# Another table of order offsets for a list-scheduled kernel: a delta-rule recurrence followed by two MLPs

## The chip, the cores and the metric

The kernel runs on one core of a Trainium2 chip. The metric is the device time of one execution in microseconds (us). Engines are called as the profile calls them: PE (TensorE), DVE (VectorE), ACT (ScalarE), POOL (GpSimd) and SP (SyncE, which issues most DMAs).

## The reference

For each of 4 batches and 8 heads a state of 40 x 40 is carried over 768 time steps; the outputs of all heads side by side are the 3072 tokens of width 320 that go through two MLPs:

```python
for t in range(S):
    y[:, :, t] = np.einsum('bhd,bhde->bhe', rt, state)
    Sa = np.einsum('bhde,bhe->bhd', state, at)
    state_decay = state * wt[:, :, None, :] - np.einsum('bhd,bhe->bhde', Sa, bt)
    state = state_decay + np.einsum('bhd,bhe->bhde', vt, kt)
...
x = attn_out.transpose(0, 2, 1, 3).reshape(B * S, H * D)      # 3072 x 320
h = x @ w_in                                                  # 320 x 2048
g = np.where(h >= 1, h, np.where(h <= -1, 0, (h + 1) ** 2 / 4))
x = g @ w_out
g = x @ w_gate                                                # 320 x 1536
out = (g / (1 + np.exp(-g)) * (x @ w_val)) @ w_out2
```

## The kernel before

Time is cut into 12 chunks of 64 steps. A unit n is one chunk of one batch, 48 in all: n = 4 * chunk + batch. The work is described as tasks; each belongs to a stage, which has a letter:

- **d** (`decay_tasks`, 3 groups of 4 chunks): running products of w and their reciprocals, stored to DRAM.
- **p** (`p_tasks`, per unit): scales a, r, k, b by these, splits them into high and low halves, transposes them, forms the chunk's products (matmuls of L889) and stores a part of them as `lsd` (L910).
- **i** (`inv_tasks`, per chunk): reloads `lsd` of all four batches as tile `ub` (L950) and solves the triangular system by 62 small steps on DVE, alternately L961 and L966, then stores the result as `tsd` (L991). Here it is called the solve.
- **m** (`m_tasks`, per unit): loads the solve's result as tile `tt`, forms the corrections (matmuls of L1103, L1110), the output and the new state, and hands the output over as `x` by a DMA transpose (L1019) into the tokens of the chunk (`mx<-x`). Chunk c needs the state of chunk c - 1.
- **a** and **b** (`in1`, `in2`, `outp`): the first and the second MLP, per chunk 8 and 6 pieces; matmuls of L1240 (into `ph`) and L1307 (into `po`).
- **w** and **v** (`wpiece`): weights of the first and of the second MLP; a piece is loaded (L639), unpacked on DVE from 64-bit floats (L644, L648, L654) and split on ACT and POOL or DVE. **z** is some padding on POOL, **o** the last output products.

Nothing loops on the chip: `Plan.run` writes out every engine's order beforehand. `forward` is a list scheduler: an engine that is free takes, among the tasks that are ready, the one with the smallest priority (a time in us); it never leaves an engine free while a task is ready on it. It has a cost for each task, a count of buffers, and a model of the DMA queue: a DMA isn't taken while the modelled queue is more than `lim` + 1.3 us ahead. `backward` does the same from the end, and gives each task the latest time at which it may start; that time is the next priority. So:

```python
bias = [b + self.offset(self.nudge, t) for t, b in zip(self.tasks, bias)]
for n in range(self.rounds):
    plan = self.forward(prio)
    ...
    if n < self.rounds - 1:
        back = self.backward([-s - c for s, c in zip(plan[1], cost)])
        prio = [plan[0] - s - c + b for s, c, b in zip(back, cost, bias)]
best = self.forward([x + self.offset(self.last, t) for x, t in zip(good, self.tasks)])
```

An offset is looked up twice: by stage and unit (`by_chunk`) and by stage and number of the task within its unit (`by_step`); `nudge` acts in every round, `last` once, at the end. A larger offset puts a task behind others that are ready at the same time. On the chip there is no priority: each engine and each DMA queue does its instructions in the order that came out, and waits at semaphores.

Of the kernel before, what the change touches and what calls it, by code (L numbers as in the profile page):

```python
# [15 lines left out]
class Plan:  # L16
# [10 lines left out]
    def __init__(self):  # L27
        self.tasks, self.made, self.pools, self.slots = [], {}, {}, {}
        self.bias, self.unit, self.nudge, self.last = 0.0, ["z", 0, 0], ({}, {}), ({}, {})
        self.lim, self.rounds, self.loose = 1.97, 5, ()  # L30
# [38 lines left out]
    def forward(self, prio):  # L69
# [56 lines left out]
        now, dma, events, done, starts, out = 0.0, 0.0, [], 0, [0.0] * len(ts), []  # L126
        held = {"DVE": 0.0, "Pool": 0.0}
        win, at_win, work, cold = 4096 / 1200, 0, {}, True
        while done < len(ts):
            started = True  # L130
            while started:
                started = False
                for eng in self.ENGINES[:5]:
# [7 lines left out]
                    while any(heaps):  # L141
                        heap = min((h for h in heaps if h), key=lambda h: h[0])
                        i = heap[0][1]
                        t = ts[i]
# [13 lines left out]
                        end = now + t["cost"]  # L158
# [3 lines left out]
                        if eng == "PE":  # L162
# [3 lines left out]
                            if cold:  # L166
                                end = now + t["cost"] * t["slow"]
# [16 lines left out]
                        if t["dma"]:  # L184
                            heapq.heappush(events, (end, -1))
                            dma = max(dma, begin) + t["dma"]
                            end = dma + 2.16
                        else:
                            end += t["lat"]
# [30 lines left out]
    def backward(self, prio):  # L220
# [16 lines left out]
        def lat(t):  # L237
            return 0.99 + t["dma"] if t["dma"] else t["lat"]
# [107 lines left out]
def tile_recurrence__then__gated_mlps(  # L346
# [1000 lines left out]
    def by(tables):  # L1347
# [23 lines left out]
    })  # L1371
    by_step = by({
# [37 lines left out]
    })  # L1410
    by_step = by({
# [178 lines left out]
```

## Time and profile before

| what | us |
|---|---|
| runs shown | 1070.62, 1068.70, 1068.02 (median 1068.7) |
| the profiled execution | 1071.23, of which the span from first to last instruction is 1069.5 |
| PE busy in the span | 879.1 (82%) |
| POOL, ACT, DVE busy | 778.7, 777.5, 658.3 |
| bytes moved by DMA | 147.93 MB, 138 GB/s on average |

A time of a run is some 1.7 us longer than the span. The rows further below are from the profiled execution.

### The profile page before, as it was taken

To read this page: it belongs to the slowest core of one execution; us is meant where nothing else is said; L and a number is where in the kernel's file an instruction comes from. 1 tells how busy PE (TensorE), PEld (TensorE's weight loads), DVE (VectorE), ACT (ScalarE), POOL (GpSimd) and SP (SyncE) were. 2 spreads that over 40 slices of the span, in tenths; PEclk is the share of its full clock that TensorE was granted. 3 is DMA by queue.
4 is the path that set the end of the run, shared out by engine and by line. 5 is a ranking of instruction groups with operands and counts; after the bars stand their busy time and mean duration, and the time that the engine had idled before them with its cause. 6 is when DMAs were issued, how large, how long until landed. Compare 5 with 4: busy or idle time off the path is not lost.

```text
span 1069.5 us, 28784 instructions
## 1 busy us (share of the span) xinstructions
PE 879.1 (82%) x10944; PEld 729.8 (68%) x10944; DVE 658.3 (62%) x1733; ACT 777.5 (73%) x1442; POOL 778.7 (73%) x996
## 2 busy tenths in 40 slices
PE   0331232955986998999999999999999999999998
PEld 0321222734775887887888888888788888888887
DVE  8789896797868375493583846837558385331111
ACT  1694666896986887888878969879698884744322
POOL 4587868786898888978888879888889764533222
PEclk9999985977998999999999999999999999999999
DMA  7976769879899678777686695957878753110000
GB/s 226 208 178 183 209 154 209 200 157 208 186 205 168 134 147 142 151 151 107 148 156 153 138 163 129 163 125 142 143 161 155 110 108 66 51 34 20 9 9 25
DMA packets 386194, 147.93 MB, mean 138 GB/s; under 512 B 344536, under 2 KB 362776, under 8 KB 386056
## 3 DMA queue, kind: packets, MB, share of 16 engines
q1 hardware_dynamic: 367706, 138.50, 62.4%
q10 hardware_dynamic: 18350, 7.61, 4.0%
q8 instruction: 85, 1.39, 0.6%
q14 instruction: 53, 0.43, 0.1%
HBM read 78.25 MB, written 21.52 MB: 93 GB/s over the span
## 4 chain that ended last, share of the span: by engine, by line
PE 55%; DVE 18%; DMA 11%; ACT 7%; POOL 5%; issue 3%; SPq 1%; ACTq 0%; DVEq 0%; POOLq 0%
PE ph L1240 29%; PE po L1307 18%; DMA mx<-x 3%; DVE pg L966 2%; DMA ub<-lsd 2%; DVE ub L961 2%; PE pg L1195 2%; PE px L1092 2%; PE px L1103 1%; DVE px L644 1%; DVE px L648 1%; PE px L1110 1%; DVE wo L654 1%; DVE vss L572 1%; POOL mx L570 1%
## 5 line engine op out<-in xcount | busy, mean ns | idle before, releaser
L1307 PE MATMUL po<-wo,mx 128*128 128x320 f16 x2016 | 310.8, 302 | 2.0 <-POOL mx L570 2.0
L570 POOL TENSOR_TENSOR mx<-mx 128x512 f16<-128x512 f32 x168 | 193.8, 1159 | 123.4 <-ACT mx L1260 112.0
L1307 PEld LDWEIGHTS <-mx 128*128 128x128 f16 x2016 | 190.9, 98 | 70.3 <-POOL mx L570 3.7
L1240 PE MATMUL ph<-mx,w 128*128 128x256 f16 x1536 | 192.1, 278 | 14.3 <-DMA mx<-x 10.8
L1240 PEld LDWEIGHTS <-w 128*128 128x128 f16 x1536 | 150.1, 100 | 39.3 <-issue 12.5
L1276 DVE SCALAR_TENSOR_TENSOR mx<-ph,mx 128x512 f32<-128x512 f32 x96 | 66.2, 689 | 146.9 <-ACT mx L1273 145.9
L1240 PE MATMUL ph<-x2t,wv 128*128 128x256 f16 x1152 | 142.2, 272 | 0.0
L1240 PE MATMUL ph<-x2t,wg 128*128 128x256 f16 x1152 | 140.8, 272 | 0.7 <-ACT mx L1287 0.7
L1260 ACT CAST mx<-mx 128x512 f16<-128x512 f32 x168 | 101.4, 612 | 42.1 <-DVE mx L1290 26.1
L1240 PEld LDWEIGHTS <-wg 128*128 128x128 f16 x1152 | 109.3, 98 | 14.8 <-issue 0.8
L1240 PEld LDWEIGHTS <-wv 128*128 128x128 f16 x1152 | 109.5, 98 | 13.0
L966 DVE TENSOR_TENSOR pg<-pg,ub 128x126 f32<-128x126 f32 (+22 forms) x372 | 96.0, 258 | 9.1
L961 DVE SCALAR_TENSOR_TENSOR ub<-ub,pg 128x126 f32<-128x126 f32 (+22 forms) x372 | 91.8, 247 | 15.8 <-DMA ub<-lsd 5.7
L1290 DVE SCALAR_TENSOR_TENSOR mx<-ph,mx 128x512 f32<-128x512 f32 x72 | 49.5, 688 | 77.1 <-PE ph L1240 66.6
L1272 ACT ACTIVATE mx<-ph 128x512 f32<-128x512 f32 x96 | 56.9, 592 | 41.4 <-PE ph L1240 34.0
L576 POOL TENSOR_TENSOR ldp<-ldp 128x640 f32<-128x640 f32 (+1 forms) x46 | 69.9, 1527 | 5.1 <-ACT ldp L856 3.8
L572 DVE SCALAR_TENSOR_TENSOR vss<-px,vss 32x320 f16<-32x320 f32 x90 | 43.6, 484 | 42.4 <-ACT vss L1135 39.4
L1287 ACT ACTIVATE mx<-ph 128x512 f32<-128x512 f32 x72 | 42.8, 595 | 36.0 <-PE ph L1240 35.2
L1135 ACT ACTIVATE vss<-px 32x640 f16<-32x640 f32 x90 | 61.1, 690 | 6.1 <-PE px L1103 3.6
L572 DVE SCALAR_TENSOR_TENSOR xs<-px,xs 32x320 f16<-32x320 f32 x89 | 42.6, 483 | 36.4 <-ACT xs L1121 34.6
L570 POOL TENSOR_TENSOR wt<-qf,wt 128x512 f16<-128x512 f32 x44 | 50.9, 1157 | 19.2 <-ACT wt L1181 18.1
L1273 ACT ACTIVATE mx<-mx 128x512 f32<-128x512 f32 x96 | 60.5, 630 | 3.0
(237 smaller groups left out, 1714.0 us busy)
## 6 DMA issues: line engine op xcount, KB each, us to landing
ldp<-in_kb_dram SPq DMA_DIRECT2D x21, 320.0 KB
ldv<-in_v_dram SPq DMA_DIRECT2D x21, 320.0 KB
ub<-lsd SPq DMA_DIRECT2D x23, 256.0 KB
ldp<-in_ar_dram SPq DMA_DIRECT2D x18, 320.0 KB
wo<-in_wo_dram SPq DMA_DIRECT2D x14, 320.0 KB
out_dram<-mx SPq DMA_DIRECT2D x24, 160.0 KB
waf<-was SPq DMA_DIRECT2D x23, 160.0 KB
ldp<-was SPq DMA_DIRECT2D x22, 160.0 KB
```

The costliest lines, as they stand in the source:

```text
L570: e.tensor_tensor(out=out, in0=x, in1=hi, op=ALU.subtract)
L572: e.scalar_tensor_tensor(out=out, in0=x, scalar=scale, in1=hi, op0=ALU.mult, op1=ALU.subtract)
L576: e.tensor_tensor(out=out, in0=x, in1=y, op=ALU.mult)
L961: v_.scalar_tensor_tensor(out=t, in0=L()[:, j, j + 1:].unsqueeze(1).to_broadcast([128, nm, ni]), scalar=-(2.0**-10), in1=m[:, 0:nm, j:j + ...
L966: v_.tensor_tensor(out=m[:, 0:nm, j + 1:], in0=m[:, 0:nm, j + 1:], in1=t, op=ALU.add)
L1135: s_.activation(out=hi2(G("vss", key)[z]), in_=two(hd(G("px", key))[32 * hf:32 * hf + 32]), func=AF.Copy, scale=-(2.0**-10))
L1240: t_.matmul(out=ps, lhsT=wts[:, wi, fs], rhs=xT[:, xi, :], start=(i == 0), stop=(i == len(plan) - 1))
L1260: T("ACT", c_s(512) - 0.04, lambda: s_.copy(out=G("g", key)[:, 0], in_=u2(key)), r=[(key, "u")], w=[(key, "gh")], use=U + GG, p=p)
L1272: s_.activation(out=u2(key), in_=ps2(key), func=AF.Relu, scale=2.0**-8, bias=1.0)
L1273: s_.activation(out=u2(key), in_=u2(key), func=AF.Square, scale=2.0**3)
L1276: T("DVE", c_v(512, True), lambda: v_.scalar_tensor_tensor(out=u2(key), in0=ps2(key), scalar=2.0**8, in1=u2(key), op0=ALU.max, op1=ALU.min ...
L1307: t_.matmul(out=ps, lhsT=g[:, x, f, 128 * tt:128 * tt + 128], rhs=wo[:, 2 * i + f, y, :], start=(n == 1 and f == 0 and m == 0), stop=(n == ...
```

## The change

The two tables of offsets, `nudge` and `last`, are replaced in full, and four numbers of the planner change. Tasks, their instructions and the cost that the planner takes for each stay as they are, so the program issues the same operations on the same engines (a plain DMA can come from SP or ACT, as before), in another order. Of the tables the lines below are those of the stages spoken of later; the rest, and both `by_step` tables, are replaced in the same way.

```diff
-        self.lim, self.rounds, self.loose = 1.97, 5, ()
+        self.lim, self.rounds, self.loose = 0.93, 2, ()
...
-                            end = dma + 2.16
+                            end = dma + 2.13
...
-            return 0.99 + t["dma"] if t["dma"] else t["lat"]
+            return 1.05 + t["dma"] if t["dma"] else t["lat"]
...
     by_chunk = by({
-        "a": {0: -1.35, 1: -1.12, 2: -0.89, 3: -0.66, 4: -0.43, 5: -0.2, 6: 0.03, 7: 0.26, 8: 0.49, 9:
-            0.72, 11: 3.5},
-        "b": {0: 1.42, 1: 1.31, 2: 1.21, 3: 1.09, 4: 0.98, 5: 0.87, 6: 0.77, 7: 0.65, 9: 1.65, 10: 0.33,
-            11: 22.69},
-        "d": {0: 4.91, 1: 0.22, 2: 0.14},
-        "i": {0: -29.34, 1: -13.04, 2: -12.55, 3: -14.73, 4: -12.76, 5: -18.16, 6: -17.61, 7: -11.81, 8:
-            -9.63, 9: -10.04, 10: -14.05, 11: -9.06},
-        "m": {9: 0.08, 10: 0.08, 11: 0.08, 12: 0.08, 40: -5.78, 45: -0.28, 46: 0.54, 47: 2.88},
...
-        "p": {0: -0.1, 1: -0.07, 2: -0.05, 3: -0.04, 4: -0.01, 5: 0.01, 6: 0.02, 7: 0.05, 8: 0.07, 9:
-            0.1, 10: 0.11, 11: 0.13, 12: 0.16, 13: 0.18, 14: 0.2, 15: 0.22, 16: 0.24, 17: 0.27, 18:
...
-        "v": {0: -5.36, 1: -5.09, 2: -4.81, 3: -4.54, 4: -4.28, 5: -4, 6: -3.73, 7: -3.46, 8: -3.18, 9:
-            -2.92, 10: -2.65, 11: -2.37, 12: -2.1, 13: -1.83, 14: -1.55, 15: -1.29, 16: -1.01, 17:
-            3.74},
...
+        "a": {0: 7.83, 1: 7.65, 2: 7.68, 3: 7.49, 4: 7.06, 5: 7.33, 6: 6.68, 7: 6.49, 8: 5.94, 9: 6.11,
+            10: 7.98, 11: 5.44},
+        "b": {0: 12.01, 1: 10.99, 2: 10.71, 3: 10.42, 4: 10.09, 5: 9.78, 6: 9.5, 7: 8.93, 8: 2.44, 9:
+            9.89, 10: 13.19, 11: 20.43},
+        "d": {0: -0.4, 1: -0.21, 2: -5.81},
+        "i": {0: 1.32, 1: -6.72, 2: -4.4, 3: 0.58, 4: 6.85, 5: -1.09, 6: -0.93, 7: -4.48, 8: 16.67, 9:
+            -2.48, 10: 26.07, 11: 17.27},
+        "m": {0: -0.98, 1: -0.84, 2: -0.7, 3: -1.59, 4: -0.42, 5: -0.26, 6: -0.16, 7: -0.02, 8: -2.92,
+            9: -1.14, 10: 0.39, 11: 0.53, 12: -0.08, 13: 1.39, 14: 0.95, 15: -0.35, 16: 1.22, 17: 1.35,
...
+        "p": {0: 14.35, 1: 11.23, 2: 11.5, 3: 11.28, 4: 9.91, 5: 9.94, 6: 11.9, 7: 9.51, 8: 10.73, 9:
+            8.22, 10: 10.53, 11: 9.4, 12: 10.37, 13: 15.11, 14: 10.19, 15: 10.1, 16: 10.03, 17: 9.94,
...
+        "v": {0: -4.69, 1: 3.52, 4: -0.75, 5: -2.29, 6: -3.81, 7: -5.32, 8: -6.81, 9: -8.61, 10: -9.88,
+            11: -12.21, 12: -12.96, 13: -14.5, 14: -16.22, 15: -17.73, 16: -19.27, 17: -26.95},
...
     by_chunk = by({
-        "d": {0: 7.57, 1: -3.33, 2: -1.8},
-        "i": {0: -6.38, 1: -0.07, 2: 11.5, 3: -1.04, 4: -35.75, 5: -26.27, 6: -0.34, 7: -0.98, 8:
...
+        "d": {0: 1.14, 1: 0.54, 2: -5.13},
+        "i": {0: -1.72, 1: -2.84, 2: -22.62, 3: -8.62, 4: -10.97, 5: 5.06, 6: 21.81, 7: 1.27, 8: -10, 9:
...
```

Summed over the two `by_chunk` tables (before, then after): stage **a**, chunks 0 to 3: -1.4, -1.2, -0.9, -0.7, then 8.4, 9.5, 7.7, 9.8. Stage **p**, units 8 to 15: 1.6, -2.1, 2.6, -0.2, 1.8, 1.5, 0.5, -0.9, then 10.4, 8.0, 9.5, 9.3, 18.8, 10.6, 9.9, 9.1. Stage **m**, units 8 to 11: 2.5, 4.1, 0.2, 0.1, then -4.7, -0.3, 0.4, -2.9. Stage **i**, chunks 0 to 5: -35.7, -13.1, -1.1, -15.8, -48.5, -44.4, then -0.4, -9.6, -27.0, -8.0, -4.1, 4.0. Stage **v**, pieces 12 to 17: -2.8, -3.3, -3.9, -4.2, -0.3, -0.8, then -16.5, -17.9, 5.6, -19.3, -22.7, -24.3. Stage **d**, group 0: 12.5, then 0.7.

## Rows read from the trace of the kernel before

**Rows 1.** Stages: us busy (count) of PE, PEld, DVE, ACT, POOL; clock, DMA share, GB/s.
```profile
0.00:184.00 184.00, 43.04 (x640) 36.33 (x641) 150.45 (x418) 110.86 (x189) 130.34 (x256) 0.91 0.78 195
184.00:350.00 166.00, 128.10 (x1573) 100.72 (x1570) 136.51 (x333) 137.43 (x263) 135.98 (x158) 0.88 0.89 186
350.00:900.00 550.00, 541.78 (x7092) 455.23 (x7091) 334.13 (x918) 459.01 (x863) 458.41 (x529) 1.00 0.74 140
900.00:1069.50 169.50, 166.17 (x1649) 137.48 (x1647) 37.22 (x65) 70.18 (x130) 54.02 (x55) 1.00 0.10 25
```
**Rows 2.** The chain that ended last, in order of time: start us, us, what.
```profile
241.41 9.18 DMA mx<-x
...
332.94 6.91 DMA mx<-x
339.89 5.32 PE ph L1240 x32
...
409.14 5.95 DMA mx<-x
415.13 5.30 PE ph L1240 x32
...
552.86 4.51 DMA mx<-x
...
1057.79 3.49 PE ph L1240 x32
1061.28 4.91 PE po L1307 x36
```

**Rows 3.** Timeline of PE, where a chunk's MLP or its corrections begin.
```profile
184.27 2.94 PE L1240 MATMUL ph<-mx,w 128*128 128x256 f16 x16
...
250.63 7.55 PE L1240 MATMUL ph<-mx,w 128*128 128x256 f16 x48 [4.87 <-DMA mx<-x]
...
263.11 0.37 PE L1103 MATMUL px<-xs,tt 96*32 96x40 f16 x8
...
304.51 0.39 PE L889 MATMUL pg<-art,kbT 120*128 120x64 f16 x8
...
360.30 0.57 PE L1103 MATMUL px<-xs,tt 96*32 96x40 f16 x16
```

**Rows 4.** DVE busy with L961 alone, in the stretches of five solves.
```profile
69.70:102.10 32.40, 7.54 (x31) 1.00 0.64 163
115.50:160.00 44.50, 7.56 (x31) 0.91 0.61 173
204.60:244.00 39.40, 7.52 (x31) 0.79 0.75 181
317.90:346.30 28.40, 7.56 (x31) 0.82 1.02 183
...
529.70:556.60 26.90, 7.56 (x31) 1.00 0.89 163
```

**Rows 5.** Groups of DVE instructions in the third of these stretches, 204.6 to 244.
```profile
L966 DVE TENSOR_TENSOR pg<-pg,ub 128x126 f32<-128x126 f32 (+21 forms) x30 | 7.8, 259 | 0.5
...
L654 DVE SCALAR_TENSOR_TENSOR wo<-wo,px 128x512 int32<-128x512 int32 (+1 forms) x6 | 3.6, 593 | 0.1
L648 DVE SCALAR_TENSOR_TENSOR px<-wo,px 128x512 int32<-128x512 int32 (+1 forms) x5 | 3.2, 634 | 0.0
L644 DVE TENSOR_SCALAR px<-wo 128x512 int32<-128x512 int32 (+1 forms) x5 | 3.1, 629 | 0.0
```

**Rows 6.** SP's own timeline: the store of the third solve's result.
```profile
249.01 3.52 SPq L991 DMA_DIRECT2D tsd<-ub  x2
```

**Rows 7.** The chain ahead of the fourth solve: start us, us, what.
```profile
307.86 4.66 DMA lsd<-gf
...
313.12 4.80 DMA ub<-lsd
```

**Rows 8.** The same view around the second chunk's handover.
```profile
241.00:251.00 10.00, 1.36 (x12) 0.76 (x11) 9.47 (x26) 4.86 (x11) 6.26 (x8) 0.50 1.11 210
251.00:300.00 49.00, 45.93 (x539) 37.20 (x537) 40.00 (x74) 42.80 (x81) 38.16 (x42) 0.96 0.88 189
300.00:333.00 33.00, 23.58 (x327) 19.17 (x326) 24.73 (x68) 28.58 (x58) 30.04 (x35) 0.95 0.96 205
```

164 rows, old and new, of tables (by_chunk, by_step) are left out of this document.

## The prediction

> **What bounds the kernel now.** I read the busy time by stage first. From 350 us to the end PE is idle for 8.2 of 550 us and 3.3 of 169.5 us; before that for 141 of 184 us and 38 of 166 us [rows 1]. So after 350 us the program is a queue of matmuls with almost no hole, and no order can take more than some 11 us out of it. That this queue runs at PE's pace shows at its end in the chain of waits: 32 matmuls of L1240 in 3.49 us and 36 of L1307 in 4.91 us [rows 2], 109 and 136 ns each; the 3840 and 2016 of them that the page counts are 693 us of the span. What an order can win lies ahead of 350 us: when the first chunks of tokens arrive.
>
> The same chain, read for what PE waits for at the turn of a chunk, names the handover `mx<-x` each time [rows 2]. The first MLP begins chunk 0 at 184.3, chunk 1 at 250.6, chunk 2 at 339.9 and chunk 3 at 415.1 us [rows 2, 3]: distances of 66, 89 and 75 us. By [rows 1] PE is the bound later; the chunk that comes after 89 us is the outlier, and the clock is hurt around it too (0.88 on average from 184 to 350 us, [rows 1]).
>
> Why chunk 2 is late is read by going back from its first correction matmul at 263.1 us [rows 3]. It needs the solve of chunk 2, which ran from 204.6 to 244.0 us [rows 4], 19.1 us ahead; for chunk 3 the same distance is 14.0 us (346.3 to 360.3) [rows 3, 4]. The 62 steps of a solve are 15.4 us of DVE (7.6 for L961, 7.8 for L966) [rows 4, 5], but the solve of chunk 2 was spread over 39.4 us, where later ones take 26.9 to 28.4 [rows 4]. What stood between its steps is largely unpacking of weights: 9.9 us of L644, L648 and L654 [rows 5]. Chunk 3 is fed in a like way: `lsd<-gf` of its last unit at 307.9, `ub<-lsd` at 313.1, and the solve at 317.9 us [rows 4, 7].
>
> **The change, part by part.** No instruction is added or taken away, so the 693 us of MLP matmuls and every engine's busy sum stay. Each part is worth what it does to those handovers.
>
> *Start, up to 184 us.* Stage d, group 0, comes forward by 11.7 us of priority, the solve of chunk 0 loses 35 us of it. The planner never leaves DVE free while something is ready, so another task slips into the gap behind a step whatever the priorities are. Bounds from the solves: the first one takes 32.4 us and could take 26.9 (-5.5) or, like the second, 44.5 (+12.1) [rows 4]. I take 0, since both signs have a reason here.
>
> *Solve of chunk 2.* Its offset goes from -1.1 to -27.0, and units 8 to 11 of stage m from between 0.1 and 4.1 to between -4.7 and 0.4, while stages a and p go back by 8 to 11 us. So the stages that feed chunk 2's handover are preferred on all engines. Bounds: -12.5 (39.4 to 26.9) and +5.1 (39.4 to 44.5) [rows 4]. Against the full gain stands that the last pieces of stage v (12, 13 and 15 to 17) come forward by 14 to 24 us, and their unpacking is what fills this very stretch. I take -6, about half of the better end, nearer to the fourth solve than to the second.
>
> *The store and reload behind it.* On SP the two stores of the solve's result took until 252.5 us (249.0 + 3.52) [rows 6], 8.5 us behind its end. With `lim` at 0.93 the planner holds DMAs back until its modelled queue is shorter by 1.04 us, so an urgent one is passed by fewer of the loads. Bounds: -5.1 (19.1 to 14.0) and 0; I take -1, the difference in `lim`, the row nearest to what is changed.
>
> *The handover transposes.* `mx<-x` took 9.18 and 6.91 us for chunks 1 and 2, 5.95 and 4.51 for chunks 3 and 5 [rows 2]; from 241 to 251 us the DMA engines had no free time (share 1.11) [rows 8]. Bounds: both like the shortest, -7.1, or both like the longest, +2.3. I take -1, by the same reasoning on `lim`. The new figures 2.13 and 1.05 shift modelled times by 0.03 and 0.06 us and I cost them at nothing, as I do `rounds`: fewer rounds change what the offsets are added to, and its effect is that of the offsets.
>
> *Chunks 3 to 5.* PE waits at 409.1 and 552.9 us for a handover again [rows 2], so a chunk 2 that is 8 us earlier pays only if those are earlier too. I count 0 here, that is, they follow: POOL and ACT are busy for 458 and 459 of 550 us [rows 1], which leaves a sixth of their time, some 36 us over the 220 us from 340 to 560, to do 8 us sooner what feeds them. Where this fails is the third rival.
>
> *The end.* Behind the last matmul only an eviction and a store are left, at most the 3.3 us in which PE is idle after 900 us [rows 1]; larger offsets of the last products change nothing there.
>
> Sum: 0 - 6 - 1 - 1 + 0 = -8 us. Against the profiled execution that is 1069.5 - 8 = 1061.5 us of span, 1063.2 us as a time; that execution (1071.23) is 2.5 us over the median of the runs shown, so against the median of 1068.7 it is 1060.7 us. A measurement of this kernel tells about 0.3% from no change, 3.2 us.
>
> **The rivals.** (1) *More of it.* The first solve and that of chunk 2 both come down to the shortest row: -5.5 - 12.5 = -18, 1050.7 us. For it: 38 us of idle PE from 184 to 350 us, and a clock of 0.88 [rows 1], so there is that much to have. Against it: the same DVE work must still be done by then, and DVE is busy for 137 of 166 us.
>
> (2) *Given back at chunk 3.* Chunk 2 comes earlier, chunk 3 does not: PE drains its queue and waits at 409 us for what it gained before. 1068.7 us. For it: PE already stands there until `mx<-x` lands at 415.1 [rows 2], without any reserve. Against: the sixth of free time above.
>
> (3) *Slower: chunk 3 starved by stage p.* Units 12 to 15 of stage p get offsets of 9 to 19, where m has about none and v is at -17 to -24. They feed `lsd<-gf` of chunk 3, which is on the chain at 307.9 us [rows 7] right behind the last product of stage p at 304.5 us [rows 3]; the solve behind it takes 28.4 us already, so it can't catch up [rows 4]. From the first us by which it is later, chunk 3's handover at 415 us is later by as much. Its price is that of the lag against m, 9 to 11 us for three of the four units, less the 1 to 2 us of the DMA terms: +8, 1076.7 us. Against it: the offsets are added to latest start times, and what is on the chain has the earliest of these.
>
> (4) *The clock.* When chunk 1 had to be waited for, PE was at the lower level (granted 0.50 from 241 to 251 us, busy for 1.4 of 10 us) [rows 8], and the first 48 matmuls behind took 7.55 us [rows 3] where 48 x 109 ns are 5.2. If the new order breaks the matmuls from 251 to 333 us up, they fall to that level in part: 69.5 us of busy PE at 0.95 to 0.96 [rows 8] would be 75.4 at 0.88, the mean from 184 to 350 us [rows 1], and 132.7 at 0.50 [rows 8]. I take the first, the nearer row: +6, 1074.7 us. The Trainium skill's page "TensorE: Matmul & The Clock Gate", section "HAM oscillation — how this bites in real kernels", says that waits between bursts make the array fall back to the slow clock, so that each burst starts cold; by that rule moving stages a behind m, with the MLP's matmuls in shorter bursts, speaks against this change, and the time would be this rival's. The trace agrees with it at 250.6 us, by the 7.55 us above. I give it little, because the matmuls of 251 to 300 us, broken up by waits as they are, still ran at 0.96 [rows 8].
>
> **How the numbers follow.** Forecast 0.42, rival 1 0.15, rival 2 0.16, rival 3 0.24, rival 4 0.03. Faster by over 0.3%: 0.42 + 0.15 = 0.57; within: 0.16; slower: 0.24 + 0.03 = 0.27. As both signs hold much, the forecast's own range is 1054 to 1066 us (the solve of chunk 2 at its best, or half of my value with the DMA terms at nothing). The range over the cases reaches from 1047, which leaves out the part of rival 1 in which the DMA terms come on top, to 1078, which leaves out those of rivals 3 and 4 in which a second handover slips too or more of the stretch runs at the lower level: about 0.15 in all.
>
> **What would show it.** Right: the first matmuls of chunk 2 at about 332 instead of 339.9 us, its solve in 34 us or less, chunk 3 at about 407, and as little idle PE after 350 us as now. Given back: chunk 2 earlier, chunk 3 still at 415. Rival 3: `lsd<-gf` of chunk 3 after 308 us and the wait at 409 us longer. Rival 4: a clock below 0.9 from 251 to 333 us. The forecast is wrong altogether if the gain or loss lies before 184 us, where I put nothing, or after 560 us.

## The result and the profile after

The kernel after takes 1059.45 us (median of 6 runs, 1055.21 to 1063.74), the kernel before 1069.66 us beside it (6 runs, 1068.02 to 1074.30): a ratio of 0.9886, interval 0.986 to 0.9913. So it is faster, by 10 us of the medians (9 to 15 us by the interval). The execution that was profiled after is the slowest of its six (1063.74 us, span 1061.6); against the span of before (1069.5) it shows 7.9 us.

The stages, busy us (count) of PE, PEld, DVE, ACT, POOL, then clock, DMA share and GB/s, in the kernel after:

```profile
0.00:184.00 184.00, 48.53 (x708) 40.89 (x709) 152.03 (x421) 116.14 (x199) 132.99 (x253) 0.65 0.78 194
184.00:350.00 166.00, 130.87 (x1604) 103.37 (x1602) 135.65 (x335) 141.81 (x270) 141.20 (x170) 0.93 0.86 194
350.00:900.00 550.00, 540.41 (x7058) 453.86 (x7057) 332.22 (x913) 451.77 (x848) 451.85 (x521) 0.99 0.73 138
```

Against [rows 1] the long middle stretch is as full as it was; PE has run 99 matmuls more by 350 us (2312 for 2213). What moved is when the chunks arrive. The timeline of PE of the kernel after, where a chunk's MLP or its corrections begin (in brackets what PE waited for, and how long):

```profile
177.47 1.88 PE L1240 MATMUL ph<-mx,w 128*128 128x256 f16 x8
...
235.63 1.89 PE L1240 MATMUL ph<-mx,w 128*128 128x256 f16 x8 [8.99 <-DMA mx<-x]
239.34 0.42 PE L1103 MATMUL px<-xs,tt 96*32 96x40 f16 x8 [1.82 <-DMA tt<-tsd]
...
324.83 1.91 PE L1240 MATMUL ph<-mx,w 128*128 128x256 f16 x16 [0.83 <-ACT mx L1287]
...
400.04 1.91 PE L1240 MATMUL ph<-mx,w 128*128 128x256 f16 x16
...
478.69 1.58 PE L1240 MATMUL ph<-mx,w 128*128 128x256 f16 x13
```

Chunk 0 comes 6.8 us sooner than in [rows 3], chunk 1 15.0, chunk 2 15.1 (339.89 to 324.83) and chunk 3 15.1 (415.13 to 400.04). Chunk 4 stood in the kernel before at:

```profile
486.84 2.34 PE L1240 MATMUL ph<-mx,w 128*128 128x256 f16 x20 [0.19 <-DMA mx<-x]
```

So it comes 8.1 us sooner, and that is what is left at the end. Two things are to be explained: where 15 us came from, and where 7 of them went between chunks 3 and 4.

**Where they came from.** DVE busy with L961 alone, in the stretches of the third and the fourth solve, kernel after:

```profile
188.00:223.60 35.60, 7.66 (x31) 0.97 0.85 206
304.00:334.70 30.70, 7.61 (x31) 1.00 0.97 208
```

Beside [rows 4] the solve of chunk 2 starts at 188.0 instead of 204.6 us (-16.6) and lasts 35.6 instead of 39.4 (-3.8). From its end to the first corrections it is 15.7 instead of 19.1 us (-3.4); the corrections are thus 23.8 us sooner. From there to the chunk's MLP it is 85.5 instead of 76.8 us (+8.7). Sum: -15.1. The largest term is the start of the solve, which the prediction did not look at.

The way back from that start leads to 131 us. SP's timeline shows the store `lsd<-gf` of the chunk's last unit and the load `ub<-lsd` with which the solve begins, first before, then after:

```profile
191.31 2.19 SPq L910 DMA_DIRECT2D lsd<-gf  x2
...
198.41 1.18 SPq L950 DMA_DIRECT2D ub<-lsd  x2
```

```profile
177.93 0.80 SPq L910 DMA_DIRECT2D lsd<-gf  x2
...
182.04 1.43 SPq L950 DMA_DIRECT2D ub<-lsd  x2
```

The store waits for stage p, and stage p's unit 9 for one of its buffers: `kbs` is written by ACT at L872 once PE has read the old one at L1195, in the product that gives the outputs of stage m's unit 1. PE's timeline of the kernel before, then of the kernel after (L818 are transposes, L1171 and L1195 products of stage m, L889 the grams of stage p):

```profile
145.59 1.03 PE L818 MATMUL po<-mx,vss 128*128 128x128 f16 x8 [5.22 <-DVE vss L572]
146.41 0.63 PE L1171 MATMUL po<-art,vsT 120*128 120x64 f16 x8
146.86 0.62 PE L889 MATMUL pg<-art,kbT 120*128 120x64 f16 x8
...
150.49 0.57 PE L1195 MATMUL po<-kbs,mx 128*128 128x40 f16 x16 [1.95 <-ACT mx L1181]
151.81 0.37 PE L1195 MATMUL po<-kbs,mx 128*128 128x40 f16 x8 [0.76 <-DVE mx L570]
```

```profile
131.41 0.59 PE L1171 MATMUL po<-art,vsT 120*128 120x64 f16 x8
...
137.88 1.04 PE L818 MATMUL po<-mx,vss 128*128 128x128 f16 x8 [2.05 <-DVE vss L572]
138.94 0.96 PE L1195 MATMUL po<-kbs,wt 128*128 128x40 f16 x24
139.73 0.59 PE L889 MATMUL pg<-art,kbT 120*128 120x64 f16 x8
```

In the kernel before, unit 1's L1171 stood behind the transposes of unit 2, for which PE waited 5.2 us for DVE; its own input had been copied by ACT (L821) by 132 us. After, it runs 15 us sooner and the output product 11.6 us sooner (138.94 for 150.49). ACT refills `kbs` behind it, before and after:

```profile
152.72 0.72 ACT L872 ACTIVATE kbs<-ldp 128x640 f16<-128x640 f32 x1
```

```profile
139.96 0.74 ACT L872 ACTIVATE kbs<-ldp 128x640 f16<-128x640 f32 x1
```

Once unit 9 has its `kbs`, the tile `ldp` is free, into which units 10 and 11 are loaded: SP issues the first of these loads (L838) at 155.56 us before and at 143.69 after. The grams of units 9, 10 and 11 come 8.6, 15.7 and 13.8 us sooner (160.31, 180.45 and 189.20 us before). So the link shown here is the larger part of the 13.4 us at the store (191.31 to 177.93), and some is added behind it.

**Where 7 us went.** SP's timeline of the kernel after at chunk 3, then PE's:

```profile
430.22 0.36 SPq L1040 DMA_DIRECT2D ldv<-in_v_dram  x1
431.04 0.48 SPq L950 DMA_DIRECT2D ub<-lsd  x1
431.70 1.25 SPq L807 DMA_TRANSPOSE vsT<-vss  x1
```

```profile
441.65 0.61 PE L1171 MATMUL pg<-art,vsT 120*128 120x64 f16 x8 [4.32 <-DMA vsT<-vss]
```

A transpose for which PE waits is issued right behind a load of 320 KB and one of 256 KB (ACT's queue issues another 256 KB at 431.85), and in the chain of waits it takes 9.91 us (431.70 to 441.61). PE stands for 4.3 us, and then runs at the lower level for a while (windows of the kernel after):

```profile
431.00:442.00 11.00, 6.68 (x124) 5.66 (x123) 4.32 (x8) 7.74 (x15) 9.49 (x11) 0.92 1.01 135
442.00:446.00 4.00, 4.00 (x28) 2.47 (x26) 2.60 (x9) 1.00 (x3) 1.16 (x1) 0.50 0.32 71
```

### The profile page after: what moved, and what is told of

Its sections match the earlier page's. It is cut to its first block, busy times and chain, and to the rows that moved or that the text cites. A ratio compares the mean times of both kernels' runs of the same rounds, so it can differ in the third digit from the quotient of the medians.

```text
span 1061.6 us, 28722 instructions
## 1 busy us (share of the span) xinstructions
PE 878.0 (83%) x10944; PEld 729.0 (69%) x10944; DVE 656.5 (62%) x1733; ACT 778.6 (73%) x1442; POOL 778.0 (73%) x996
## 4 chain that ended last, share of the span: by engine, by line
PE 60%; DVE 17%; ACT 7%; DMA 7%; POOL 4%; issue 4%; SPq 1%; ACTq 0%; POOLq 0%; DVEq 0%
PE ph L1240 31%; PE po L1307 20%; PE pg L1195 2%; DVE ub L961 2%; DVE pg L966 2%; DMA vsT<-vss 2%; PE px L1092 2%; PE px L1103 2%; DVE px L644 2%; PE px L1110 1%; DVE px L648 1%; POOL mx L570 1%; DVE wo L654 1%; DMA tsd<-ub 1%; DMA tt<-tsd 1%
## 5 line engine op out<-in xcount | busy, mean ns | idle before, releaser
L1240 PEld LDWEIGHTS <-w 128*128 128x128 f16 x1536 | 147.4, 99 | 44.3 <-issue 13.3
L1240 PE MATMUL ph<-x2t,wg 128*128 128x256 f16 x1152 | 144.9, 276 | 2.3 <-DVE mx L1276 2.0
L961 DVE SCALAR_TENSOR_TENSOR ub<-ub,pg 128x126 f32<-128x126 f32 (+22 forms) x372 | 92.0, 247 | 16.5 <-DMA ub<-lsd 6.1
L1103 PEld LDWEIGHTS <-tt 96*128 96x128 f16 (+1 forms) x768 | 28.3, 97 | 46.7 <-issue 26.3
```

The lines of the kernel that those rows point to most:

```text
L961: v_.scalar_tensor_tensor(out=t, in0=L()[:, j, j + 1:].unsqueeze(1).to_broadcast([128, nm, ni]), scalar=-(2.0**-10), in1=m[:, 0:nm, j:j + ...
L1103: t_.matmul(out=out, lhsT=lhsT, rhs=xs[:, h], start=False, stop=(h == H - 1), skip_group_check=True)
L1240: t_.matmul(out=ps, lhsT=wts[:, wi, fs], rhs=xT[:, xi, :], start=(i == 0), stop=(i == len(plan) - 1))
```

## The experiments

Most of them set the two orders beside each other as fixed lists and splice them; the planner is not run anew, since its offsets hold for one plan only: of the 16 ways to mix the old and the new values of the four numbers, the new tables give an order with the four new ones alone. So what the tables bring without the numbers was not tried. The splice follows for T = 110 us, T being a time of the plan; `old` and `new` are the two plans, in runs 6 and 7 they change places, and every buffer is chosen as its own plan chose it. Here and in the later runs, a step that can't have its buffer or its input yet is passed by until it can:

```diff
+    a, b = new, old
+    first = [x for x in a[2] if a[1][x[0]] < 110.0]
+    done = {i for i, _ in first}
+    order = first + [x for x in b[2] if x[0] not in done]
```

**1. new110_old and 2. new180_old** (T = 110 and 180): is it the start, or stage p?

> New order for all tasks that the new plan starts before 110 us, the order of before for the rest. Theory A (the gain is made between 120 and 240 us, where units 9 to 11 of stage p and with them the solve of chunk 2 come sooner): nothing won yet, chunk 2's first matmul at 338 to 342 us as before, time 1066 to 1073 us, ratio to before 0.997 to 1.004. Rival B (the gain comes from the start, stage d and the padding): chunk 2 at 330 us or earlier, 1062 us or less, ratio below 0.993.

> New order up to 180 us, the order of before for the rest. Theory A: the solve of chunk 2 begins near 188 instead of 204.7 us, so most of the lead is there; chunk 2's first matmul at 326 to 333 us, time 1055 to 1063 us, ratio 0.987 to 0.994. Rival C (the lead is made behind 180 us, by fewer DMAs ahead of the handovers and less unpacking inside the solve of chunk 2): chunk 2 at 336 us or later, ratio above 0.996.

Measured: 1079.4 us (ratio 1.0069, 1.0045 to 1.0093), chunk 2 at 345.7; and 1076.99 us (1.0055, 1.0037 to 1.0073), chunk 2 at 342.7. Both are slower than the kernel before, the first also than either theory had it, so the first 110 us bring no gain by themselves. The second is the instructive miss: the grams of stage p for chunk 2 ran at 137.6 to 173.2 us, as soon as in the kernel after, and the solve still started at 209. Its SP timeline shows why:

```profile
175.75 0.80 SPq L910 DMA_DIRECT2D lsd<-gf  x2
...
202.51 1.23 SPq L950 DMA_DIRECT2D ub<-lsd  x2
```

The store is there at 175.8, but the load behind it keeps the place that the old order gave it in the queue, behind stores and weight loads, and is issued 26.8 us later (4.1 in the kernel after). What comes sooner is worth nothing as long as its consumer's load keeps its place.

**3. new240_old, 4. new300_old and 5. new340_old** (T = 240, 300, 340): how much of the stretch is needed?

> New order up to 240 us, so with the whole of chunk 2's solve, the order of before for the rest. Theory A, narrowed by the cut at 180 us (stage p of chunk 2 was 16 us sooner there, but the load for its solve kept its old place in the queue, and nothing was won): with the solve in its new place it begins near 188 us and chunk 2's corrections near 240; chunk 2's first matmul at 323 to 332 us, time 1056 to 1063 us, ratio 0.986 to 0.994. Rival F (the whole stretch to 340 us has to be in the new order, since stage m of chunk 2 keeps its old places): chunk 2 at 335 us or later, ratio above 0.996.

> The order of after up to 300 us of the plan, that of before behind. Theory A (the seam at 240 us cost what it did because PE found an eviction on DVE that the order of before had put elsewhere, a hole of 16.2 us behind the seam; nothing in the content of 240 to 300 us is lost by a later seam): corrections of chunk 2 at 237 to 242, its MLP at 322 to 328, time 1057 to 1064 us, as with the seam at 340. Theory F (the whole stretch up to the handover of chunk 2 is needed, its end too): the MLP of chunk 2 at 334 to 345 and 1068 to 1078 us, as with the seam at 240.

> New order up to 340 us, the order of before for the rest. Theory A with its second part (the new order is 15 us ahead at chunks 2 and 3 and gives 7 us back at chunk 4, where a transpose stands behind the load of the next solve): chunk 2 at 324 to 326, chunk 4 at 470 to 474 us (before 486.8, after 478.7), time 1052 to 1057 us, ratio 0.984 to 0.989, so better than the change itself by 3 to 7 us. Rival D (the lead can't be kept whatever comes behind, because chunk 4's work needs that time): chunk 4 at 478 us or later, 1058 to 1062 us.

Measured: 1076.97 us (1.008, 1.0049 to 1.011), 1065.28 us (0.996, 0.994 to 0.9981) and 1059.14 us (0.990, 0.9868 to 0.9931); chunk 2 at 343.6, 336.1 and 321.7. With the new order up to 340 us and the old one behind, the whole gain is there: it lies ahead of the MLP of chunk 2. It is no better than the change itself, against theory A: chunk 4 came at 473.5 us as expected, but of the lead of 18.2 us at chunk 2 only 12.6 were left at chunk 3 (402.5). With an earlier seam it is lost in part or wholly although the solve ended at 221 to 223 us in all three. At 240 a hole opens right behind the seam, where PE waits for an eviction on DVE (PE's timeline of new240_old):

```profile
259.77 5.05 PE L1240 MATMUL ph<-mx,w 128*128 128x256 f16 x32 [16.20 <-DVE mx L1276]
```

With the seam at 300 the corrections of chunk 2 come at 236.7 us, no later than after (239.3), and its MLP is still late. So an early solve is not enough; each seam also has a price of its own, which these runs do not separate from it.

**6. old340_new** (the other way round, T = 340): does the late part bring something?

> Order of before up to 340 us, the new order for the rest. Theory A: no lead to start with, chunk 2 at 339 to 341 us, and the transpose behind the load costs its 4 to 7 us at chunk 4: time 1069 to 1077 us, ratio 1.000 to 1.008. Rival E (the gain is made in the steady part, behind 340 us): 1064 us or less, ratio below 0.996.

Measured: 1068.78 us, 0.9979 (0.996 to 0.9998), chunk 2 at 338.4. The late part is worth some 2 us by itself (0.2 to 4 by the interval). Neither theory holds: the cost expected at chunk 4 did not come (485.3 us, with no wait for that transpose over 1.9 us), and the gain isn't there either.

**7. old110_new** (old up to 110, new behind):

> The order of before up to 110 us of the plan, that of after behind. Theory A (the first 110 us bring nothing by themselves, the gain is made between 110 and 340 us): the MLP of chunk 2 at 321 to 328 us, time 1052 to 1061 us. Theory B (the start is needed for it after all, or a seam costs some us wherever it is): the solve of chunk 2 at 195 us or later, its MLP at 333 or later, 1066 to 1080 us.

Measured: 1060.99 us, 0.9911 (0.9878 to 0.9945); solve of chunk 2 at 190.6, chunk 2 at 326.5. The start isn't needed either; and this seam cost next to nothing. What is left is 110 to 340 us of the plan.

**8. old_fewbits**: the step that the prediction named, by itself. The order of before, without the unpacking of six pieces of weights that falls into the solve of chunk 2:

```diff
-              lambda q=q: bits(q), r=[(key, q)],
+              lambda q=q: bits(q) if key not in SKIP else q < 2 or v_.memset(u(), 0.0), r=[(key, q)],
```

> The order of before; six weight pieces whose unpacking on DVE stands between the steps of chunk 2's solve are not unpacked (a memset of the result in place of the three or four instructions), so the second MLP's first pieces are computed from zeros. The forecast's step (the solve of chunk 2 is stretched by unpacking, and its end sets chunk 2's handover and all that follows): solve from 39 to 29 to 33 us, chunk 2's first matmul at 330 to 334 instead of 339.9, time 5 to 9 us less, ratio 0.991 to 0.996. Rival 2 of the forecast (given back at chunk 3): chunk 2 sooner, chunk 3's first matmul at 413 to 416 as before, ratio 0.998 to 1.002.

Measured: 1070.43 us, 1.0015 (0.9992 to 1.0038). L961 alone in the stretch of that solve:

```profile
204.30:240.50 36.20, 7.35 (x31) 0.79 0.73 186
```

It starts where it did in [rows 4] and is 3.2 us shorter, not by the 6 to 10 expected. Chunk 2 comes at 336.0 and chunk 3 at 409.5 in this profile, that of the second fastest of ten executions, and the median does not move; rival 2's ratio is met, but not by its mechanism, since chunk 3 is not late. A solve that is shorter by about as much as the change made it (3.8 us) brings nothing measurable by itself: unpacking is not what the gain hangs on.

**9. new_late16**: the start of the solve, by itself. The order of after, with the solve's steps, loads and stores 16 us later in the list, and what depends on them as much later as no slack absorbs (one unit of stage m, by up to 13 us):

```diff
+        if t["unit"][:2] == ("i", 2):
+            delay[i] = max(delay[i], 16.0)
...
+            delay[j] = max(delay[j], delay[i] - max(0.0, new[1][j] - end))
+    order = sorted(new[2], key=lambda x: new[1][x[0]] + delay[x[0]])
```

> The order of after, but the whole third solve (with its loads and stores) is placed 16 us later in the plan, and whatever depends on it as much later as the plan's slack does not absorb. Theory A (the solve of chunk 2 starts 16.7 us sooner, and this is what makes the MLP of chunk 2 15 us sooner): solve at 202 to 206 us as in before, the first corrections of chunk 2 at 250 to 256, the MLP of chunk 2 at 333 to 340, time 1062 to 1070 us. Theory G (the solve was not what set it: between its end and the handover of chunk 2 there is slack, since the 80 us of stage m and the evictions on DVE and ACT set the pace): the solve moves as far, the MLP of chunk 2 stays at 321 to 327, time 1051 to 1058 us.

Measured: 1068.08 us, 0.9986 (0.9962 to 1.001): the gain in time is gone. PE's timeline of this kernel at chunk 0, chunk 1, the corrections of chunk 2 and its MLP:

```profile
175.03 1.88 PE L1240 MATMUL ph<-mx,w 128*128 128x256 f16 x8
...
234.53 1.86 PE L1240 MATMUL ph<-mx,w 128*128 128x256 f16 x8 [10.31 <-DMA mx<-x]
...
250.42 0.45 PE L1103 MATMUL px<-xs,tt 96*32 96x40 f16 x8 [4.46 <-DMA tt<-tsd]
...
333.34 1.91 PE L1240 MATMUL ph<-mx,w 128*128 128x256 f16 x16 [0.84 <-ACT mx L1287]
```

Chunks 0 and 1 are as soon as after; the solve runs from 201.2 to 236.7, so 13.2 of the 16.6 us are taken back. Chunk 2 is back by 8.5 us, and the time by 8.6 (by the ratios, 1.0%). So the start of the solve is the larger part of the lead at chunk 2, but not all of it: chunk 2 is still 6.5 us sooner than in the kernel before, and chunk 3 6.7 (408.4). What the rest rests on, the 9 and 16 us by which chunks 0 and 1 are sooner or something else, the run doesn't tell. It is given back where the kernel after gives back 7 us: chunk 4 begins at 486.3 us (486.8 before), behind a wait for the same transpose.

```profile
450.79 0.61 PE L1171 MATMUL pg<-art,vsT 120*128 120x64 f16 x8 [5.35 <-DMA vsT<-vss]
```

**10. new_q13**: the last link of the way back. The order of after, with the last sixteen steps of stage m's unit 1 (its product of L1171, the output product behind that, the new state and the handover) 13 us later:

```diff
-        if t["unit"][:2] == ("i", 2):
-            delay[i] = max(delay[i], 16.0)
+        if t["unit"][:2] == ("m", 1) and t["unit"][2] >= 21:
+            delay[i] = max(delay[i], 13.0)
```

> The order of after, but the product of stage m's unit 1 that gives its outputs (and what follows from it) is placed 13 us later in the plan, about where it stood in the order of before; all else keeps its place, save what can get no buffer or input by then. Theory A (the solve of chunk 2 starts sooner since this product frees a buffer of stage p sooner: the last link of the way back): the product at 148 to 153 us, the grams of stage p for the last three units of chunk 2 later by 6 us or more, the solve at 194 to 204, the MLP of chunk 2 at 329 to 338, time 1060 to 1069 us. Theory H (the buffer is one of several things that come sooner, and stage p has slack behind it): the solve at 190 or sooner, the MLP of chunk 2 at 327 or sooner, time 1051 to 1058 us.

Measured: 1070.38 us, 0.9999 (0.9976 to 1.0022). ACT's and PE's timelines of this kernel, and SP's:

```profile
149.12 0.74 ACT L872 ACTIVATE kbs<-ldp 128x640 f16<-128x640 f32 x1 [2.78 <-PE po L1195]
```

```profile
148.12 0.97 PE L1195 MATMUL po<-kbs,wt 128*128 128x40 f16 x24
...
190.72 1.87 PE L1240 MATMUL ph<-mx,w 128*128 128x256 f16 x8
...
338.18 1.91 PE L1240 MATMUL ph<-mx,w 128*128 128x256 f16 x16 [0.83 <-ACT mx L1287]
```

```profile
190.74 0.80 SPq L910 DMA_DIRECT2D lsd<-gf  x2
...
195.07 1.24 SPq L950 DMA_DIRECT2D ub<-lsd  x2
```

ACT waits for just this product, the store comes 12.8 us later than after, the solve at 201.7 and chunk 2 at 338.2. Sixteen steps out of place, with what had to make way for them, undo the change. But this isn't the buffer alone. The grams of units 9, 10 and 11 come at 153.85, 171.07 and 188.94 us, that is 2.1, 6.3 and 13.6 us later than after. What unit 11 loses on top shows in the chain of waits: the handover of the same outputs is late too (issued at 170.18 us, after at 150.28), ACT and POOL make the next `x` behind it, and POOL gets to `ars` of unit 11 only then (its transpose is issued at 177.34 us, after at 167.41).

```profile
170.18 5.03 DMA mx<-x
175.23 0.48 ACT x L1005
...
176.53 0.79 POOL ars L570
```

Chunk 0 falls back with that handover as well (190.7). So the run shows that the outputs of unit 1 decide when the solve can start, by the buffer and by the handover together; it doesn't show that the buffer alone does.

**11. new_again and 12. new_vst**: is the wait at 441 us an accident of one run, and does it cost what was given back? The first is the order of after once more; in the second three loads (`ldv` of stage m's units 20 and 21, both halves of `ub<-lsd` of chunk 5) go behind the transpose for which PE waits:

```diff
+    late = [at["m", 20, 0], at["i", 5, 0], at["i", 5, 1]]
+    order = [x for x in order if x[0] not in late]
+    n = 1 + [i for i, _ in order].index(at["m", 17, 18])
+    order[n:n] = [(i, "SP") for i in late]
```

> The changed kernel's own order, instruction for instruction, as the yardstick for the next one and as a second trace of it. Theory A: 1057 to 1062 us, chunk 2's first matmul at 321 to 326 us, and PE waiting for the transpose at about 437 to 442 us again. If what the first trace showed at chunk 4 was an accident of that execution, that wait is under 1 us here and chunk 4 begins at 472 us or earlier.

> The new order with three loads (v of units 20 and 21, and the two halves of chunk 5's tile for the solve) put behind the transpose of unit 17, nothing else moved. Theory A (the give-back at chunk 4 is this transpose standing behind these loads): the transpose lands within 5 us instead of 9.9, the wait of PE at 441 us is gone, chunk 4's first matmul comes 3 to 7 us sooner, time 3 to 6 us under the kernel beside it in this call, ratio to before 0.982 to 0.986. Rival D (chunk 4 is bound by the work of all engines): the wait moves elsewhere, chunk 4 as late as before, no difference over 2 us.

Measured: 1053.83 us (1052.9 to 1062.2; 0.9882, 0.9848 to 0.9917) and 1051.11 us (1048.74 to 1051.83; 0.9836, 0.9807 to 0.9865). The first is faster than expected, though its ratio is that of the kernel after (0.9886); the second is 2.7 us under it by the medians, a little less than the 3 to 6 expected. In this second trace of the same order chunk 2 comes at 321.9 and chunk 3 at 397.2 us, 3 us sooner than in the first, so 3 us between two traces can be scatter. The wait is there in the first run as well:

```profile
438.29 0.41 PE L1171 MATMUL pg<-art,vsT 120*128 120x64 f16 x8 [3.74 <-DMA vsT<-vss]
```

and gone in the second (SP's timeline, then PE's at the same product and at chunk 4):

```profile
429.44 1.25 SPq L807 DMA_TRANSPOSE vsT<-vss  x1
430.82 0.50 SPq L1040 DMA_DIRECT2D ldv<-in_v_dram  x1
431.43 1.13 SPq L950 DMA_DIRECT2D ub<-lsd  x2
```

```profile
436.38 0.40 PE L1171 MATMUL pg<-art,vsT 120*128 120x64 f16 x8
...
470.26 1.91 PE L1240 MATMUL ph<-mx,w 128*128 128x256 f16 x16
```

Chunk 4 comes at 470.3 instead of 473.7 in new_again. From chunk 3 to chunk 4 it is now 70.7 us, against 76.5 in new_again, 78.7 in the kernel after and 71.7 before: nothing is given back there any more. Three loads moved behind one transpose make the fastest version of all, 1.6% below the kernel before; the ranges of these two runs do not overlap, though the intervals of their ratios do by a little.

## Why the prediction was right in its number and wrong in its reason

The direction, the size (1060.7 us predicted, 1059.45 measured, both against a median before of about 1069) and the place of the bound were right. The way to it was not, and by the prediction's own test: it called itself wrong altogether if the gain lay before 184 us, and the links that the way back found lie at 131 to 182.

- **What bounds it.** Right. The MLP queue after 350 us is as full as it was, and earlier chunks 0 and 1 are no gain in time by themselves: run 9 keeps them and loses the gain. An earlier chunk 2 pays only as far as chunk 4 is earlier too; in run 9 6.5 us at chunk 2 brought nothing.
- **Start, 0.** This is the step that failed. What it put at nothing is the largest term. The prediction priced the first solve, whose stretch did not change (70.2 to 101.9 us after), and took the start of the third as given. It began 16.6 us sooner. That "another task slips into the gap behind a step whatever the priorities are" was said of DVE; the gap that mattered stood on PE at 145.6 us, where a product was queued behind transposes that had to wait, and on SP in the load's place. [rows 4] had the start beside the length; the way back ought to have gone on from the start, to the wait ahead of it.
- **Solve of chunk 2, -6.** Mis-sized: -3.8; at 35.6 us it is also longer than the 34 that the prediction named as a sign of being right. In that stretch L644, L648 and L654 took 5.7 us instead of the 9.9 of [rows 5], but in run 8 taking such work away brought nothing measurable.
- **Store and reload, -1.** -3.4 from the solve's end to the corrections; the share of `lim` in it was not tried.
- **Handover transposes, -1.** Chunk 2's wait for `mx<-x` became one of 0.83 us for ACT; that of chunk 1 grew to 8.99 from 4.87. The term that the prediction lacked is stage m of chunk 2: +8.7 us from the corrections to the MLP, in which DVE, ACT and POOL are busy for 136, 142 and 141 of 166 us. That these set its pace is argued from those shares, and no run was made for it.
- **Chunks 3 to 5 follow, 0.** Right for chunk 3 (-15.1), wrong for chunk 4 (-8.1): 7.0 us given back. Rival 2 had the mechanism one chunk too early, and the wait was `vsT<-vss` in stage m, not the handover. Run 12 shows the wait, and chunk 4 3.4 us sooner without it.
- **End, 0.** Right: 8.1 us at chunk 4 are 7.9 at the end.

So -8 came out of a gain of 15 with 7 given back, not of -6 - 1 - 1: that the size fits is luck. Rival 3 (chunk 3 starved by stage p) did not happen: the solve of chunk 3 began at 304.0 instead of 317.9 us [rows 4], so stage p, whatever its offsets, was not late there. Rival 4 decided nothing over the whole stretch (clock 0.93 for 0.88 in [rows 1], and 0.94 from 251 to 333 us, where it was to be below 0.9). But it is a second part of the loss at 441 us, where the granted clock fell to 0.50, the lower of its two levels (1.2 GHz), once PE had stood for 4.3 us; in run 12, without that wait, it is 1.00 from 431 to 446 us. By the section "HAM oscillation — how this bites in real kernels" of the Trainium skill's page "TensorE: Matmul & The Clock Gate" a wait between bursts costs in two ways, as idle time and as a cold start behind it. The windows at 442 us agree.

On run 12, the Trainium skill's page "Trainium Kernel Development and Optimization", section "Key Constraints", says that DMAs of all issuing queues run on the same 16 engines and interleave. The trace of the kernel after agrees at 431 to 442 us, where the DMA engines had no free time (share 1.01): the transpose was issued behind two loads of its own queue, and ACT's queue issued a third 0.15 us later.

## What to carry to other kernels

When a late step is found, go back from its start as well as along its length: the 39 us of the solve were in plain sight, and the 17 us were in what it waited for, two engines and a queue further up. In a program of in-order queues a result that comes sooner is worth nothing until the load that fetches it is moved too, and one product placed behind an instruction that must wait can, with what follows from it, hold up a chunk 190 us later. Then look for what is given back: a single transpose issued behind loads that nobody needs yet undid part of the gain, and three moved loads brought some of it back.

## What was not expected of the hardware

The clock of the first 180 us differed between two executions of the very same order. Windows of the profiled execution after, then of new_again:

```profile
49.00:181.00 132.00, 39.15 (x606) 32.95 (x607) 109.34 (x289) 94.87 (x167) 107.62 (x194) 0.51 0.76 187
```

```profile
49.00:181.00 132.00, 40.69 (x616) 34.18 (x616) 110.37 (x291) 95.72 (x169) 108.85 (x195) 1.00 0.76 188
```

In a stretch where PE is busy for less than a third, one ran at the lower level and the other at the upper one. It hardly matters there: chunk 0 began at 177.5 and 176.5 us. It does mean that the mean clock of a whole span (0.923 and 0.987) is no measure of how good an order is.
